# Filler products of ones in TensorE's early waits of a block linear-attention and gated-MLP kernel

## The chip, the core and the metric

The kernel runs on one NeuronCore of a Trainium2 chip. The metric is the device time of one execution in microseconds (us), less being better. Five runs of the kernel before give a median of 153.36 us (153.28 to 153.47).

## What is computed

Two stages in a row. The first is linear attention with decay over 4 batches, 8 heads, 768 tokens and head size 64, in blocks of 64 tokens: inside a block, masked and decayed scores times v; from earlier blocks, q times a running 64x64 state per head. The second is an MLP with a spatial gate on the attention's output (4 x 768 x 512):

```
for b in range(nb):
    intra = einsum('bhic,bhjc->bhij', qb, kb) * Dmask;  intra = einsum('bhij,bhjd->bhid', intra, vb)
    inter = einsum('bhid,bhde->bhie', qb * lam_pow, kv_state)
    out[:, :, sl] = intra + inter
    kv_state = lam_block * kv_state + einsum('bhsd,bhse->bhde', kb * rev_pow, vb)
...
h = maximum(x @ w_in, 0);  u, v = halves of h
v_n = (v - mean) / sqrt(var + 1e-6)
out = (u * (w_spatial @ v_n + b_spatial)) @ w_out
```

## The kernel before, in words

The work is cut into 12 steps n of 256 tokens, three to a batch. For each step q, k and v are loaded (512 KB each, into 3 buffers in turn), cast to bf16, and k and q are transposed on TensorE (TK, TQ, L302) and copied out of PSUM as kT and qT (EK, EQ). Scores are SC (L331), masked on VectorE by MK (L335). AV.n.0 and AV.n.1 (L368 and L377) form the attention output of step n: products of q with the state copied to SBUF, and products of v with the masked scores. KV.n.c (L347) adds block half c of step n to the running state, which lives in the first 256 columns of PSUM bank 7 (`SB`), and SS.n.c (L353, a copy whose line in the profile is its helper's, L170 on ScalarE and L172 on VectorE) copies that state to `s_sb`. AV.n.1 needs the copy SS.n.0. EX evicts AV as xT. Then follow the MLP's products PV (L406, the v half, with eviction EV, statistics BN, RA, RD and normalisation VN), PU (L451, the u half, eviction EU), and later PW (L473, spatial), GB and GM (the gate) and PO (L490, output).

The order of every instruction is written out by hand in the string `ORDER`: each token names a helper, its arguments and its engine (T TensorE, D VectorE, A ScalarE, P GpSimd, S SyncE; `AV.2.1.0.T` is step 2, part 1, bank 0), and each engine takes its own tokens strictly in that order. Waits between engines are made from the tiles that the instructions read and write. For PSUM they are made by bank: a product into a bank waits until an earlier reader of that bank is done, even if it read other columns. The loads of weights are put behind the arrival of certain inputs: GT (L237) is a tiny GpSimd copy that reads one element of an input and so holds GpSimd's queue until that input has landed, and the weight load follows it (WI, L241, two halves of w_in; WS, L246, two halves of w_spatial).

Lines of the order around the change, of the kernel before:

```
KV.0.1.T EX.0.0.0.A SS.0.1.D SC.1.1.2.T SC.1.0.4.T
...
AV.1.0.0.T BN.0.1.D EV.0.0.5.A LQ.4.2.S KV.1.0.T BN.0.0.D TQ.2.6.T SS.1.0.A GT.0.2.P WS.1.P KC.2.2.A
AV.1.1.0.T EQ.2.6.D KV.1.1.T EX.1.0.0.D SS.1.1.A TK.2.6.T EX.1.1.1.A RA.0.A PV.1.1.5.T
...
AV.2.0.0.T VN.1.0.A LV.3.2.S EU.1.1.5.A KV.2.0.T SS.2.0.A KC.3.2.D AV.2.1.0.T
EX.2.0.0.D EX.2.1.1.A TK.3.6.T PV.2.1.5.T
```

Of the kernel before, what the change touches and what calls it, by code (L numbers as in the profile page):

```python
# [9 lines left out]
BF16 = mybir.dt.bfloat16  # L10
# [3 lines left out]


ORDER = """
LK.0.2.S lam.A idn.P LQ.0.2.S msk.P LV.0.2.S LK.1.2.S LB.6.T pos.P mkc.D LN.6.A LQ.1.2.S LL.D KC.0.2.P LX.A
LV.1.2.S TK.0.6.T LT.0.A QC.0.2.D EK.0.6.D TQ.0.5.T LT.1.A LQ.2.2.S EQ.0.5.D GT.2.0.P WI.0.P LT.2.A SC.0.0.0.T
LK.2.2.S SC.0.1.2.T VD.0.2.P MK.0.0.0.D KC.1.2.A MK.0.1.2.D LV.2.2.S TK.1.6.T AV.0.0.0.T QC.1.2.D EK.1.6.A
KV.0.0.T TQ.1.5.T SS.0.0.D AV.0.1.0.T EQ.1.5.D KV.0.1.T EX.0.0.0.A SS.0.1.D SC.1.1.2.T SC.1.0.4.T EX.0.1.1.A  # L20
MK.1.1.2.D LK.3.2.S MK.1.0.4.D GT.2.1.P WI.1.P PV.0.1.6.T VD.1.2.D LQ.3.2.S PV.0.0.5.T EV.0.1.6.A QC.2.2.P
AV.1.0.0.T BN.0.1.D EV.0.0.5.A LQ.4.2.S KV.1.0.T BN.0.0.D TQ.2.6.T SS.1.0.A GT.0.2.P WS.1.P KC.2.2.A
AV.1.1.0.T EQ.2.6.D KV.1.1.T EX.1.0.0.D SS.1.1.A TK.2.6.T EX.1.1.1.A RA.0.A PV.1.1.5.T EK.2.6.D SC.2.1.0.T
SC.2.0.2.T EV.1.1.5.A PV.1.0.6.T MK.2.1.0.D BS.S PU.0.0.5.T RD.0.D EV.1.0.6.A BN.1.1.D GT.2.2.P WS.0.P
VN.0.1.A PU.0.1.4.T BN.1.0.D EU.0.0.5.A VD.2.2.P PU.1.0.6.T VN.0.0.A MK.2.0.2.D EU.0.1.4.A PU.1.1.5.T RA.1.A
EU.1.0.6.A RD.1.D VN.1.1.D AV.2.0.0.T VN.1.0.A LV.3.2.S EU.1.1.5.A KV.2.0.T SS.2.0.A KC.3.2.D AV.2.1.0.T
EX.2.0.0.D EX.2.1.1.A TK.3.6.T PV.2.1.5.T EK.3.6.A PV.2.0.4.T EV.2.1.5.A PU.2.0.6.T BN.2.1.D EV.2.0.4.A
LK.4.2.S WT.1.5.T BN.2.0.D EU.2.0.6.A WT.5.4.T QC.3.2.P EW.1.5.A WT.4.3.T EW.5.4.D WT.0.6.T WT.3.2.T RA.2.A
EW.4.3.D LQ.5.2.S EW.0.6.A WT.2.5.T RD.2.D TQ.3.4.T VN.2.1.D VN.2.0.A QC.4.2.D PU.2.1.6.T EW.2.5.A LK.5.2.S
EQ.3.4.D TQ.4.3.T EW.3.2.A SC.3.0.0.T EQ.4.3.D EU.2.1.6.A SC.3.1.4.T PW.0.1.1.2.T MK.3.0.0.D LV.4.2.S  # L30
PW.0.1.0.6.T VD.3.2.P MK.3.1.4.D PW.0.0.0.3.T LQ.6.2.S GB.0.1.0.6.D GB.0.1.1.2.D PW.0.0.1.5.T KC.4.2.A
GB.0.0.0.3.D GM.0.1.1.P LV.6.2.S GM.0.1.0.D AV.3.0.0.T KV.3.0.T GB.0.0.1.5.D TK.4.6.T GM.0.0.0.P SY.3.0.A
SS.3.0.A PW.0.3.1.5.T EK.4.6.A GM.0.0.1.P LQ.7.2.S PW.0.2.0.4.T GB.0.3.1.5.D QC.5.2.P GM.0.3.1.D KV.3.1.T
AV.3.1.0.T GB.0.2.0.4.D LV.5.2.S KC.5.2.A SC.4.1.2.T SC.4.0.5.T GM.0.2.0.P PW.0.3.0.4.T MK.4.1.2.D EX.3.1.1.A
VD.4.2.P EX.3.0.0.A TK.5.1.T MK.4.0.5.D LK.6.2.S SS.3.1.A TQ.5.3.T EK.5.1.A PU.3.0.0.T EQ.5.3.D QC.6.2.P
PU.3.1.6.T LK.7.2.S GB.0.3.0.4.D EU.3.0.0.A KV.4.0.T GM.0.3.0.P EU.3.1.6.D AV.4.0.0.T SS.4.0.A SC.5.1.2.T
SC.5.0.4.T SY.4.0.D LQ.9.2.S KV.4.1.T MK.5.1.2.D AV.4.1.0.T SS.4.1.A PV.3.1.6.T EX.4.0.0.A VD.6.2.P MK.5.0.4.D
EX.4.1.1.A TQ.6.0.T LV.7.2.S PU.4.1.1.T EV.3.1.6.D QC.7.2.P PU.4.0.5.T EQ.6.0.D EU.4.1.1.A LV.9.2.S BN.3.1.D
PV.4.1.6.T GT.2.5.P WO.P EU.4.0.5.D KC.6.2.A PW.0.2.1.4.T VD.5.2.P EV.4.1.6.D LK.8.2.S TK.6.5.T BN.4.1.D
PV.3.0.6.T EK.6.5.A GB.0.2.1.4.D KV.5.0.T LV.8.2.S EV.3.0.6.D AV.5.0.0.T GM.0.2.1.P SS.5.0.A SC.6.1.2.T  # L40
SC.6.0.4.T SY.5.0.D BN.3.0.D KV.6.0.T AV.5.1.0.T KC.7.2.P PV.4.0.6.T EX.5.0.0.A MK.6.0.4.D EX.5.1.1.A TK.7.0.T
RA.3.A SS.6.0.D PU.5.1.1.T EV.4.0.6.A EK.7.0.D PV.5.1.6.T BN.4.0.D EU.5.1.1.A MK.6.1.2.D TQ.7.0.T LK.9.2.S
RA.4.A EV.5.1.6.A PV.5.0.1.T QM.9.0.P BN.5.1.D PO.0.0.6.T EV.5.0.1.A QM.9.1.P RD.4.D LQ.8.2.S EQ.7.0.D
PO.0.1.5.T VN.4.0.A BN.5.0.D VD.7.2.P EO.0.0.6.A PO.0.2.4.T EO.0.1.5.A VN.4.1.D ST.0.0.S RA.5.A AV.6.0.0.T
EO.0.2.4.A KV.6.1.T SC.7.1.2.T SY.6.0.D RD.5.D SC.7.0.5.T SS.6.1.A KC.8.2.P RD.3.D AV.6.1.0.T MK.7.1.2.D
VN.5.0.A KV.7.0.T PO.0.5.4.T LV.10.2.S EX.6.1.1.A SS.7.0.A MK.7.0.5.D VN.3.1.A PO.0.3.1.T VD.8.2.P EX.6.0.0.D
KV.7.1.T DK.8.S EO.0.3.1.A AV.7.0.2.T VN.3.0.D PU.5.0.6.T SS.7.1.A SY.7.2.A KC.9.2.P VN.5.1.D PV.6.1.5.T
ST.0.1.S EU.5.0.6.D PV.6.0.1.T ST.0.3.S QM.8.1.P EV.6.1.5.D AV.7.1.2.T EV.6.0.1.D QM.8.0.P KV.8.0.T PU.6.0.6.T
EX.7.1.3.A BN.6.1.D LK.11.2.S EX.7.0.2.A VD.9.2.P PW.1.1.1.3.T BN.6.0.D SS.8.0.A EU.6.0.6.A PU.7.1.2.T RA.6.A
DQ.8.S GB.1.1.1.3.D RD.6.D PU.6.1.6.T GM.1.1.1.D VN.6.0.A LQ.11.2.S EU.7.1.2.A EO.0.5.4.D PW.1.0.1.3.T DK.9.S  # L50
EU.6.1.6.A VN.6.1.A PW.1.3.1.2.T GB.1.0.1.3.D ST.0.2.S GM.1.0.1.P PV.7.1.6.T GB.1.3.1.2.D PV.7.0.3.T
# [30 lines left out]
def kernel(  # L82
# [29 lines left out]
    def sb(shape, dt, name):  # L112
        return const.tile(shape, dt, name=name)
# [5 lines left out]
    SB = 7  # L119
# [45 lines left out]
    def bank(b, n=1):  # L165
        return ps[:, b] if n == 1 else ps[:, b:b + n]
# [338 lines left out]
    def st_o(e, bb, t):  # L505
        eng = {"S": nc.sync, "A": nc.scalar}[e]
        eng.dma_start(out=out[bb, t * P:(t + 1) * P, :], in_=o_sb[(bb * NT + t) % NO])

    ops = dict(GT=after, lam=c_lam, pos=c_pos, LB=l_b, LN=l_n, LL=l_l, LX=l_x, LT=l_t, idn=c_ident, msk=c_mask, mkc=c_mask2, WI=w_in, WS=w_sp, WO=w_out, BS=b_sp,
               LK=ld_k, LQ=ld_q, LV=ld_v, KC=k_c, QM=q_m, DK=d_k, DQ=d_q, QC=q_c, VD=v_d, TK=t_k, TQ=t_q, EK=e_k, EQ=e_q,  # L510
               SC=s_c, MK=m_k, KV=k_v, SS=s_s, AV=a_v, SY=s_y, EX=e_x, PV=p_v, EV=e_v, BN=b_n, RA=r_a, RD=r_d,
               VN=v_n, PU=p_u, EU=e_u, WT=w_t, EW=e_w, PW=p_w, GB=g_b, GM=g_m, PO=p_o, EO=e_o, ST=st_o, EH=e_h, SH=s_h)
# [34 lines left out]
```

## Time and profile before

| | before |
|---|---|
| median of 5 runs | 153.36 us |
| the profiled execution's own time | 153.62 us |
| its span, first to last instruction | 151.9 us |
| TensorE products, busy | 132.5 us (87%), 2011 recorded |
| VectorE busy | 110.7 us (73%) |
| ScalarE busy | 85.9 us (57%) |
| GpSimd busy | 71.9 us (47%) |
| mean granted TensorE clock | 0.995 |
| moved by DMA | 30.73 MB, mean 202 GB/s |
| a load of k, q or v, issue to landing | 7.1 us (median) |
| a half of w_in, issue to landing | 9.6 us (median) |

Times in the profile count from the first instruction. A timeline row holds start, duration, engine, source line, operation, output and inputs, shape and how many instructions are merged; in square brackets stands how long the engine was idle before it and what ended the wait. The duration of merged products includes the latency of the last one. "PE" is TensorE, "PEld" its weight loads, "POOL" GpSimd, "DVE" VectorE, "ACT" ScalarE. A few products are missing from the trace. The chain of waits is followed back from the last instruction to what released it, and so on to the start.

### The profile page before, as it was taken

To read this page: it belongs to the slowest core of one execution; us is meant where nothing else is said; L and a number is where in the kernel's file an instruction comes from. 1 tells how busy PE (TensorE), PEld (TensorE's weight loads), DVE (VectorE), ACT (ScalarE), POOL (GpSimd) and SP (SyncE) were. 2 spreads that over 40 slices of the span, in tenths; PEclk is the share of its full clock that TensorE was granted. 3 is DMA by queue.
4 is the path that set the end of the run, shared out by engine and by line. 5 is a ranking of instruction groups with operands and counts; after the bars stand their busy time and mean duration, and the time that the engine had idled before them with its cause. 6 is when DMAs were issued, how large, how long until landed. Compare 5 with 4: busy or idle time off the path is not lost.

```text
span 151.9 us, 4756 instructions
## 1 busy us (share of the span) xinstructions
PE 132.5 (87%) x2011; PEld 87.9 (58%) x2026; DVE 110.7 (73%) x200; ACT 85.9 (57%) x158; POOL 71.9 (47%) x73
## 2 busy tenths in 40 slices
PE   1259498969979999999999999999999999999990
PEld 1248347755855688685656756664576656556530
DVE  3467847764999689999999669976589949535611
ACT  6882237897952474565964732968351777670140
POOL 7472023800404798955888050897384020009720
PEclk9999999999999999999999999999999999999998
DMA  3999999999999996999799999675654010151055
GB/s 105 298 290 249 289 226 292 238 245 303 258 288 293 291 229 185 285 218 306 200 207 299 205 273 297 178 140 110 221 182 46 4 73 0 69 207 71 0 211 207
DMA packets 52040, 30.73 MB, mean 202 GB/s; under 512 B 9522, under 2 KB 48946, under 8 KB 52018
## 3 DMA queue, kind: packets, MB, share of 16 engines
q1 hardware_dynamic: 49488, 27.53, 69.9%
q0 software_dynamic: 2384, 2.75, 10.7%
q8 instruction: 16, 0.26, 0.8%
q10 hardware_dynamic: 146, 0.13, 0.2%
q14 instruction: 6, 0.05, 0.1%
HBM read 24.77 MB, written 6.29 MB: 204 GB/s over the span
## 4 chain that ended last, share of the span: by engine, by line
PE 63%; DMA 12%; DVE 11%; ACT 7%; issue 3%; SPq 1%; POOL 0%; ACTq 0%; DVEq 0%
PE ps L473 20%; PE ps L406 13%; PE ps L451 11%; PE ps L490 8%; DMA win_sb<-in_moe_w_in_dram 6%; DMA v_in<-in_v_dram 4%; PE ps L377 3%; DVE a_sb L335 2%; PE ps L331 2%; PE ps L302 2%; PE ps L347 2%; ACT vn L439 2%; PE ps L368 2%; ACT o_sb L170 2%; DMA out_dram<-o_sb 2%
## 5 line engine op out<-in xcount | busy, mean ns | idle before, releaser
L484 POOL TENSOR_TENSOR gT<-vsb,uT 128x384 bf16<-128x384 f32 x24 | 26.1, 1105 | 42.2 <-DVE vsb L478 41.1
L473 PE MATMUL ps<-wt_sb,vn 128*128 128x384 bf16 x192 | 33.7, 326 | 0.7 <-DVE vsb L478 0.6
L335 DVE TENSOR_TENSOR a_sb<-ps,m 128x1024 bf16<-128x1024 f32 x24 | 28.4, 1213 | 2.3 <-PE ps L331 2.2
L406 PE MATMUL ps<-win_sb,xT 128*128 128x512 bf16 x87 | 23.6, 399 | 3.6 <-DMA win_sb<-in_moe_w_in_dram 1.9
L473 PEld LDWEIGHTS <-vn 128*128 128x128 bf16 x192 | 18.5, 98 | 13.1 <-issue 0.7
L294 POOL TENSOR_TENSOR vd<-v_in,lv 128x1024 bf16<-128x1024 f32 x11 | 21.0, 1906 | 10.8 <-DVE rstd L432 9.5
L478 DVE TENSOR_TENSOR vsb<-ps,bsp 128x384 f32<-128x384 f32 x32 | 17.3, 551 | 9.6 <-PE ps L473 8.5
L451 PE MATMUL ps<-xT,win_sb 128*128 128x256 bf16 x192 | 23.9, 273 | 0.0
L421 DVE BATCH_NORM_STATS2 st<-vh 128x6 f32<-128x512 bf16 x24 | 16.5, 686 | 9.5 <-ACT vh L411 9.2
L490 PE MATMUL ps<-wout_sb,gT 128*128 128x512 bf16 x90 | 21.6, 379 | 0.5 <-issue 0.3
L451 PEld LDWEIGHTS <-win_sb 128*128 128x128 bf16 x192 | 18.4, 98 | 4.2
L170 ACT ACTIVATE o_sb<-ps 128x512 f32<-128x512 f32 (+1 forms) x20 | 11.5, 583 | 14.6 <-PE ps L490 9.9
L170 ACT ACTIVATE xT<-ps 128x512 bf16<-128x512 f32 x21 | 11.6, 592 | 7.7 <-PE ps L377 7.7
L406 PEld LDWEIGHTS <-xT 128*128 128x128 bf16 x96 | 9.1, 101 | 11.8 <-issue 3.6
L439 ACT ACTIVATE vn<-vh,nmr,rstd 128x512 bf16<-128x512 bf16 x16 | 12.8, 812 | 4.9 <-DVE nmr L433 4.9
L411 ACT ACTIVATE vh<-ps 128x512 bf16<-128x512 f32 x15 | 8.9, 593 | 11.3 <-PE ps L406 11.2
L490 PEld LDWEIGHTS <-gT 128*128 128x128 bf16 x96 | 9.1, 98 | 10.3 <-DMA wout_sb<-in_moe_w_out_dram 0.2
L411 ACT ACTIVATE uT<-ps 128x512 bf16<-128x512 f32 x20 | 11.7, 590 | 5.4 <-PE ps L451 5.4
L377 PE MATMUL ps<-a_sb,vd 64*64 64x128 bf16 x384 | 10.8, 229 | 0.1
L331 PE MATMUL ps<-qT,kT 64*64 64x128 bf16 x384 | 9.2, 233 | 0.9 <-DVE qT L315 0.9
L302 PE MATMUL ps<-ident,kc 128*128 128x128 bf16 x64 | 5.7, 242 | 4.6 <-POOL kc L174 3.5
L279 POOL TENSOR_TENSOR qc<-q_in,lqn 128x512 bf16<-128x512 f32 x7 | 7.7, 1116 | 3.3 <-issue 3.3
(68 smaller groups left out, 171.6 us busy)
## 6 DMA issues: line engine op xcount, KB each, us to landing
k_in<-in_k_dram SPq DMA_DIRECT2D x12, 512.0 KB, 7.1
q_in<-in_q_dram SPq DMA_DIRECT2D x12, 512.0 KB, 7.1
v_in<-in_v_dram SPq DMA_DIRECT2D x12, 512.0 KB, 7.1
out_dram<-o_sb SPq DMA_DIRECT2D x23, 256.0 KB, 2.2
wsp_raw<-in_moe_w_spatial_dram POOLq DMA_DIRECT2D x2, 576.0 KB, 9.3
win_sb<-in_moe_w_in_dram POOLq DMA_DIRECT2D x2, 512.0 KB, 9.6
wout_sb<-in_moe_w_out_dram POOLq DMA_DIRECT2D x1, 512.0 KB, 9.1
bsp<-in_moe_b_spatial_dram SPq DMA_DIRECT2D x1, 384.0 KB, 12.3
```

Of the source, the lines that this page charges most:

```text
L170: nc.scalar.activation(out=o, in_=i, func=AF.Copy)
L294: vec(e).tensor_tensor(out=vd[n % NCA][:, h], in0=v_in[n % NIN][:, h], in1=lv[:, n % NR, h].unsqueeze(3).broadcast_to((P, h.stop - h.start ...
L335: nc.vector.tensor_tensor(out=a_sb[n % NA][:, i].rearrange("p o w j x -> p (o w) (j x)"), in0=bank(b, 2).rearrange("p o (w y) -> p (o w) y ...
L406: nc.tensor.matmul(out=bank(b), lhsT=x[:, c, g], rhs=win_sb[:, g, DH:DFF], start=(g == 0), stop=(g == NCH - 1))
L411: nc.scalar.activation(out=o, in_=i, func=AF.Relu)
L421: nc.vector.bn_stats(out=st6[p2][:, t], in_=vh[p2][:, t])
L439: nc.scalar.activation(out=vn[p2][:, t], in_=vh[p2][:, t], func=AF.Identity, scale=rstd[p2][:, t:t + 1], bias=nmr[p2][:, t:t + 1])
L451: nc.tensor.matmul(out=pu[:, f2].rearrange("p (c x) -> p c x", c=2), lhsT=win_sb[:, g, f * P:(f + 1) * P], rhs=x[:, :, g, :], start=(g == ...
L473: nc.tensor.matmul(out=bank(b)[:, 0:HW], lhsT=vn[bb % 2][:, s, f * P:(f + 1) * P], rhs=wt_sb[:, s, i * HW:(i + 1) * HW], start=(s == 0), s ...
L478: nc.vector.tensor_tensor(out=vsb[(bb * 4 + f) % NVS][:, i * HW:(i + 1) * HW], in0=bank(b)[:, 0:HW], in1=bsp[:, i * HW:(i + 1) * HW], op=A ...
L484: vec(e).tensor_tensor(out=gT[bb % 2][:, f, cols].rearrange("p (a y m) -> p a y m", m=2, y=Q64), in0=vsb[(bb * 4 + f) % NVS][:, cols].rear ...
L490: nc.tensor.matmul(out=bank(b), lhsT=gT[bb % 2][:, f, t * P:(t + 1) * P], rhs=wout_sb[:, f, :], start=(f == 0), stop=(f == NCH - 1))
```

## The change

A tile `warm` of 128x128 bf16 is added and filled with 1.0 by one VectorE memset, ahead of the other work of VectorE. A helper WU issues n products of `warm` with itself, each with its own weight load, into columns 256 to 383 of bank 7, which nothing reads. 14 tokens of it, 152 products in all, stand in the order from the start up to step 3; nothing else in the order is moved.

```diff
+    warm = sb([P, P], BF16, "warm")
...
+    def w_u(e, n):
+        if n < 0:
+            nc.vector.memset(warm, 1.0)
+        for x in range(abs(n)):
+            nc.tensor.matmul(out=bank(SB)[:, 4 * D:4 * D + P], lhsT=warm, rhs=warm, start=(n < 0 and x == 0), stop=True,
+                             skip_group_check=True)
```

Where the tokens stand on TensorE (number of products, and what follows them there): 8 before LB.6 (the first product of the kernel, L201), 45 before TK.0, 10 before TQ.0, 12 before SC.0.0, 21 before TK.1, 4 before KV.0.0, 3 before SC.1.1, 22 before PV.0.1, 4 before KV.1.0, 4 before TK.2, 4 before PV.1.1, 4 before KV.2.0, 8 before AV.2.1 and 3 before TK.3.

More of the change, by code (lines that the diff above doesn't have):

```diff
@@ L16 @@
 ORDER = """
[L17 to L46, printed above, removed]
@@ L47 @@
-KV.7.1.T DK.8.S EO.0.3.1.A AV.7.0.2.T VN.3.0.D PU.5.0.6.T SS.7.1.A SY.7.2.A KC.9.2.P VN.5.1.D PV.6.1.5.T
-ST.0.1.S EU.5.0.6.D PV.6.0.1.T ST.0.3.S QM.8.1.P EV.6.1.5.D AV.7.1.2.T EV.6.0.1.D QM.8.0.P KV.8.0.T PU.6.0.6.T
+LK.0.2.S lam.A idn.P LQ.0.2.S msk.P LV.0.2.S LK.1.2.S WU.-8.T LB.6.T pos.P mkc.D LN.6.A LQ.1.2.S LL.D KC.0.2.P
+LX.A LV.1.2.S WU.45.T TK.0.6.T LT.0.A QC.0.2.D EK.0.6.D WU.10.T TQ.0.5.T LT.1.A LQ.2.2.S EQ.0.5.D GT.2.0.P
+WI.0.P LT.2.A WU.12.T SC.0.0.0.T LK.2.2.S SC.0.1.2.T VD.0.2.P MK.0.0.0.D KC.1.2.A MK.0.1.2.D LV.2.2.S WU.21.T
@@ new lines @@
+TK.1.6.T AV.0.0.0.T QC.1.2.D EK.1.6.A WU.4.T KV.0.0.T TQ.1.5.T SS.0.0.D AV.0.1.0.T EQ.1.5.D KV.0.1.T
+EX.0.0.0.A SS.0.1.D WU.3.T SC.1.1.2.T SC.1.0.4.T EX.0.1.1.A MK.1.1.2.D LK.3.2.S MK.1.0.4.D GT.2.1.P WI.1.P
+WU.22.T PV.0.1.6.T VD.1.2.D LQ.3.2.S PV.0.0.5.T EV.0.1.6.A QC.2.2.P AV.1.0.0.T BN.0.1.D EV.0.0.5.A LQ.4.2.S
+WU.4.T KV.1.0.T BN.0.0.D TQ.2.6.T SS.1.0.A GT.0.2.P WS.1.P KC.2.2.A AV.1.1.0.T EQ.2.6.D KV.1.1.T EX.1.0.0.D
+SS.1.1.A WU.4.T TK.2.6.T EX.1.1.1.A RA.0.A WU.4.T PV.1.1.5.T EK.2.6.D SC.2.1.0.T SC.2.0.2.T EV.1.1.5.A
@@ new lines @@
+PV.1.0.6.T MK.2.1.0.D BS.S PU.0.0.5.T RD.0.D EV.1.0.6.A BN.1.1.D GT.2.2.P WS.0.P VN.0.1.A PU.0.1.4.T BN.1.0.D
+EU.0.0.5.A VD.2.2.P PU.1.0.6.T VN.0.0.A MK.2.0.2.D EU.0.1.4.A PU.1.1.5.T RA.1.A EU.1.0.6.A RD.1.D VN.1.1.D
+AV.2.0.0.T VN.1.0.A LV.3.2.S EU.1.1.5.A WU.4.T KV.2.0.T SS.2.0.A KC.3.2.D WU.8.T AV.2.1.0.T EX.2.0.0.D
+EX.2.1.1.A WU.3.T TK.3.6.T PV.2.1.5.T EK.3.6.A PV.2.0.4.T EV.2.1.5.A PU.2.0.6.T BN.2.1.D EV.2.0.4.A LK.4.2.S
+WT.1.5.T BN.2.0.D EU.2.0.6.A WT.5.4.T QC.3.2.P EW.1.5.A WT.4.3.T EW.5.4.D WT.0.6.T WT.3.2.T RA.2.A EW.4.3.D
@@ new lines @@
+LQ.5.2.S EW.0.6.A WT.2.5.T RD.2.D TQ.3.4.T VN.2.1.D VN.2.0.A QC.4.2.D PU.2.1.6.T EW.2.5.A LK.5.2.S EQ.3.4.D
+TQ.4.3.T EW.3.2.A SC.3.0.0.T EQ.4.3.D EU.2.1.6.A SC.3.1.4.T PW.0.1.1.2.T MK.3.0.0.D LV.4.2.S PW.0.1.0.6.T
+VD.3.2.P MK.3.1.4.D PW.0.0.0.3.T LQ.6.2.S GB.0.1.0.6.D GB.0.1.1.2.D PW.0.0.1.5.T KC.4.2.A GB.0.0.0.3.D
+GM.0.1.1.P LV.6.2.S GM.0.1.0.D AV.3.0.0.T KV.3.0.T GB.0.0.1.5.D TK.4.6.T GM.0.0.0.P SY.3.0.A SS.3.0.A
+PW.0.3.1.5.T EK.4.6.A GM.0.0.1.P LQ.7.2.S PW.0.2.0.4.T GB.0.3.1.5.D QC.5.2.P GM.0.3.1.D KV.3.1.T AV.3.1.0.T
@@ new lines @@
+GB.0.2.0.4.D LV.5.2.S KC.5.2.A SC.4.1.2.T SC.4.0.5.T GM.0.2.0.P PW.0.3.0.4.T MK.4.1.2.D EX.3.1.1.A VD.4.2.P
+EX.3.0.0.A TK.5.1.T MK.4.0.5.D LK.6.2.S SS.3.1.A TQ.5.3.T EK.5.1.A PU.3.0.0.T EQ.5.3.D QC.6.2.P PU.3.1.6.T
+LK.7.2.S GB.0.3.0.4.D EU.3.0.0.A KV.4.0.T GM.0.3.0.P EU.3.1.6.D AV.4.0.0.T SS.4.0.A SC.5.1.2.T SC.5.0.4.T
+SY.4.0.D LQ.9.2.S KV.4.1.T MK.5.1.2.D AV.4.1.0.T SS.4.1.A PV.3.1.6.T EX.4.0.0.A VD.6.2.P MK.5.0.4.D EX.4.1.1.A
+TQ.6.0.T LV.7.2.S PU.4.1.1.T EV.3.1.6.D QC.7.2.P PU.4.0.5.T EQ.6.0.D EU.4.1.1.A LV.9.2.S BN.3.1.D PV.4.1.6.T
@@ new lines @@
+GT.2.5.P WO.P EU.4.0.5.D KC.6.2.A PW.0.2.1.4.T VD.5.2.P EV.4.1.6.D LK.8.2.S TK.6.5.T BN.4.1.D PV.3.0.6.T
+EK.6.5.A GB.0.2.1.4.D KV.5.0.T LV.8.2.S EV.3.0.6.D AV.5.0.0.T GM.0.2.1.P SS.5.0.A SC.6.1.2.T SC.6.0.4.T
+SY.5.0.D BN.3.0.D KV.6.0.T AV.5.1.0.T KC.7.2.P PV.4.0.6.T EX.5.0.0.A MK.6.0.4.D EX.5.1.1.A TK.7.0.T RA.3.A
+SS.6.0.D PU.5.1.1.T EV.4.0.6.A EK.7.0.D PV.5.1.6.T BN.4.0.D EU.5.1.1.A MK.6.1.2.D TQ.7.0.T LK.9.2.S RA.4.A
+EV.5.1.6.A PV.5.0.1.T QM.9.0.P BN.5.1.D PO.0.0.6.T EV.5.0.1.A QM.9.1.P RD.4.D LQ.8.2.S EQ.7.0.D PO.0.1.5.T
@@ new lines @@
+VN.4.0.A BN.5.0.D VD.7.2.P EO.0.0.6.A PO.0.2.4.T EO.0.1.5.A VN.4.1.D ST.0.0.S RA.5.A AV.6.0.0.T EO.0.2.4.A
+KV.6.1.T SC.7.1.2.T SY.6.0.D RD.5.D SC.7.0.5.T SS.6.1.A KC.8.2.P RD.3.D AV.6.1.0.T MK.7.1.2.D VN.5.0.A
+KV.7.0.T PO.0.5.4.T LV.10.2.S EX.6.1.1.A SS.7.0.A MK.7.0.5.D VN.3.1.A PO.0.3.1.T VD.8.2.P EX.6.0.0.D KV.7.1.T
+DK.8.S EO.0.3.1.A AV.7.0.2.T VN.3.0.D PU.5.0.6.T SS.7.1.A SY.7.2.A KC.9.2.P VN.5.1.D PV.6.1.5.T ST.0.1.S
+EU.5.0.6.D PV.6.0.1.T ST.0.3.S QM.8.1.P EV.6.1.5.D AV.7.1.2.T EV.6.0.1.D QM.8.0.P KV.8.0.T PU.6.0.6.T
@@ L507, in st_o @@
         eng.dma_start(out=out[bb, t * P:(t + 1) * P, :], in_=o_sb[(bb * NT + t) % NO])
-    ops = dict(GT=after, lam=c_lam, pos=c_pos, LB=l_b, LN=l_n, LL=l_l, LX=l_x, LT=l_t, idn=c_ident, msk=c_mask, mkc=c_mask2, WI=w_in, WS=w_sp, WO=w_out, BS=b_sp,
+    ops = dict(GT=after, lam=c_lam, WU=w_u, pos=c_pos, LB=l_b, LN=l_n, LL=l_l, LX=l_x, LT=l_t, idn=c_ident, msk=c_mask, mkc=c_mask2, WI=w_in, WS=w_sp, WO=w_out, BS=b_sp,
                LK=ld_k, LQ=ld_q, LV=ld_v, KC=k_c, QM=q_m, DK=d_k, DQ=d_q, QC=q_c, VD=v_d, TK=t_k, TQ=t_q, EK=e_k, EQ=e_q,
```

## Prediction

> **What bounds the kernel now.** I read the slices of the page first, then TensorE's timeline over the first 36 us, where all of the new products stand, then the chain of waits, then the landings of the inputs.
>
> The page's slices (3.8 us each) show TensorE busy in patches up to about the tenth slice, the DMA engines full there, and a granted clock that is full in every slice but the last:
>
> ```profile
> PE   1259498969979999999999999999999999999990
> PEclk9999999999999999999999999999999999999998
> DMA  3999999999999996999799999675654010151055
> ```
>
> The clock row doesn't tell the whole story. TensorE's timeline holds the same work twice:
>
> ```profile
> 15.57 1.04 PE L331 MATMUL ps<-qT,kT 64*64 64x128 bf16 x28
> 18.55 0.58 PE L406 MATMUL ps<-win_sb,xT 128*128 128x512 bf16 x1 [1.94 <-DMA win_sb<-in_moe_w_in_dram]
> 19.36 2.76 PE L406 MATMUL ps<-win_sb,xT 128*128 128x512 bf16 x6 [0.22 <-issue]
> ...
> 23.26 1.04 PE L302 MATMUL ps<-ident,qc 128*128 128x128 bf16 x8
> ...
> 25.07 0.61 PE L302 MATMUL ps<-ident,kc 128*128 128x128 bf16 x8
> 26.20 0.81 PE L406 MATMUL ps<-win_sb,xT 128*128 128x512 bf16 x3 [0.52 <-ACT xT L170]
> 26.94 0.64 PE L331 MATMUL ps<-qT,kT 64*64 64x128 bf16 x32
> ```
>
> Eight transposes take 1.04 us at 23.26 and 0.61 at 25.07; 32 score products 0.64 at 26.94 where 28 took 1.04 at 15.57. In w_in's products the pitch is (2.76 - 0.58) / 5 = 0.44 us at 19.36, against 0.22 later (4 in 1.04 us with a latency of 0.38). So TensorE works at half speed until about 24.2 us and at full speed after that. The change fills its waits so that full speed comes earlier. What that is worth depends on which of the slow work lies on the chain:
>
> ```profile
> 8.79 9.72 DMA win_sb<-in_moe_w_in_dram
> ...
> 25.04 0.38 ACT s_sb L170
> 25.43 0.50 ACT xT L170
> 25.93 0.27 issue
> 26.20 0.81 PE ps L406 x3
> ...
> 33.59 0.28 ACT s_sb L170
> 33.87 0.04 issue
> 33.91 0.31 PE ps L368 x8
> ```
>
> Up to 18.51 the chain is a transfer (v of step 0, then w_in). From 18.55 to 25.02 it is TensorE at half speed, then ScalarE and TensorE in turn, and at 33.91 AV.2.1, which waited for the state copy SS.2.0. After that the chain has no input transfer before the end: TensorE, VectorE and ScalarE only. A shift of AV.2.1 therefore goes through to the end nearly unchanged.
>
> The last view is what lands beside this chain:
>
> ```profile
> 23.33 0.18 POOL L237 COPY seen<-k_in 1x1 f32<-1x1 f32 x1 [2.49 <-DMA k_in<-in_k_dram]
> 23.37 0.38 ACT L170 ACTIVATE s_sb<-ps 128x256 bf16<-128x256 f32 x1 [0.61 <-PE ps L347]
> 23.65 1.05 ACT L170 ACTIVATE kc<-k_in 128x1024 bf16<-128x1024 f32 x1
> ```
>
> k of step 2 lands at about 23.3 (GpSimd had waited 2.49 us for it). Its cast KC.2 sits in ScalarE's queue ahead of SS.1.1, EX.1.1, RA.0 and EV.1.1. ScalarE passes 23.3 no earlier however fast TensorE is.
>
> **The change, part by part.**
>
> *The 125 products up to PV.0.1 (8, 45, 10, 12, 21, 4, 3, 22).* Price: they have the shape of the transposes, so 0.113 us each slow ((1.03 - 0.24) / 7, from eight in 1.03) and 0.055 fast (eight start 0.44 us ahead of the next eight around 54 us). At most 125 x 0.113 = 14.1 us, at least 6.9. They run in waits that the timeline shows before the work that they precede (3.47 us before TK.0, 0.40, 0.85, 1.02, then 1.94 before PV.0.1), and they may overrun: 45 x 0.113 = 5.1 us before TK.0 against 3.47 idle, 1.6 late if all are slow. That costs nothing at the end if TensorE, which was done at 16.61, still reaches PV.0.1 by 18.51; once the array is fast, the work between (some 7 us at half speed) gives back over 3 us. The memset costs VectorE some 0.2 us (0.17 for its neighbour) ahead of the wait for the mask; the eight first products end near 2.1, where LB began at 2.11. WU.3 before SC.1.1 inherits a wait for SS.0.1, since both touch bank 7; SC.1.1 then starts up to 0.6 later than now, but runs 0.4 us shorter. All of this lies before 18.51 and is covered by w_in's landing. I take 0; were the cover gone, it would be 1 to 2 us.
>
> Here the Trainium skill ("TensorE: Matmul & The Clock Gate", Part 1) bears on the gain: the array starts at half clock, turns fast after about 3.4 us of sustained work, and for modelling the ramp costs under 1% of a typical span (1.5 us here). The row differs: from 11.55 TensorE was at work nearly without a break to 16.61 and stayed slow. By the rule TensorE would be fast near 7 us; by the slowest row (dense from 18.55, fast at 24.2: 5.6 us) near 8.3. In both cases it is fast by 18.55, which is what matters.
>
> *PV.0.1 to EX.1.1, the gain.* From 18.55 to 25.02 TensorE does some 6.5 us of chain, mostly slow; at full speed it would do it in about 3.5. But KC.2 waits for k. After it: KC.2 23.33 to 24.38 (was 23.65 to 24.70), SS.1.1 at 24.3 (was 25.04, having waited 0.35 for KV.1.1), done near 24.67, EX.1.1 done near 25.2 (was 25.92). So ScalarE gains 0.75 us, not 3. TensorE gains less: the four products before TK.2 write bank 7 after KV.1.1, so in the built program the first of them carries the wait for SS.1.1; before, TK.2 waited for KC.2 only. Start 24.71, four products 0.22, eight transposes 0.44, four products 0.22: PV.1.1 at about 25.6 to 25.65, where it was 26.20. The gain is 0.55 us. EK.2 (VectorE, at 25.6) is ready for SC.2.0, so PV.1.0 keeps the 0.55, and EV.1.0 goes from 28.59 to 28.04. From there the chain is ScalarE back to back to SS.2.0, 33.59 to 33.87: 33.32 in place of 33.87. VD.2, needed by AV.2.0, ends at 29.0 whatever TensorE does (v lands at 25.7), before the 31.4 at which AV.2.0 would come.
>
> *WU.4 before KV.2.0.* 0.22 us; KV.2.0 ended near 32.74 and SS.2.0 began at 33.48, being behind ScalarE's queue: covered.
>
> *WU.8 before AV.2.1, the price.* In the built program the first of the eight carries the wait for SS.2.0, the very copy that AV.2.1 waits for (1.17 us idle in the trace). The eight are thus not in the wait but behind it, and AV.2.1, EX.2.1 and PV.2.1 are queued behind them: 8 x 0.055 = 0.44 us straight on the chain. Ends: 0.44 by the transposes' pitch, 0.78 if each weight load (98 ns in the PEld rows) counts in full. I take 0.44, the row of the same shape.
>
> *WU.3 before TK.3.* 0.17 us; PV.2.1 waits for EX.2.1, with 0.36 us of idle time before it: covered. EK.3 follows 0.1 later on ScalarE, just ahead of EV.2.1.
>
> *Sum.* AV.2.1 at 33.32 + 0.04 + 0.44 = 33.80, where it was 33.91: -0.11 us. The profiled execution took 153.62 us (span 151.9 and 1.7 around it) and would take 153.51; it lies 0.26 above the median of the runs, so against the median 153.36 - 0.11 = 153.25.
>
> **The rivals.**
>
> *Clearly faster.* ScalarE's gain of 0.75 reaches SS.2.0 in full, because PV.1.1 is released by EX.1.1 and not by the products ahead of it: -0.75 + 0.44 = -0.31, so 153.05; with a little more from looser ordering after step 3, 152.9. For it: the chain from 25.04 runs through EX.1.1. Against it: in the sum TensorE arrives 0.15 to 0.2 after EX.1.1. Chance 0.25.
>
> *Slower.* The eight products behind SS.2.0 keep their price, and the gain before them is lost on the way: SS.2.0 is held by ScalarE's full queue from 28.59, and if EV.1.0 comes no earlier (bank waits, VectorE's masks and RD.0 ahead of VN.0.1), the price stands alone: +0.44, 153.80. It decides as soon as SS.2.0 gains less than 0.13 us. Against it: each link in front is TensorE or ScalarE work that moves with the clock. Chance 0.12.
>
> *The clock doesn't hold.* With the work before k's landing done early, TensorE idles from about 22.5 to 24.7, 2.2 us; the longest idle time that the trace shows at full speed up to 60 us is 1.2. If the array fell to half speed there, the 3 us of work to PV.1.0 would take 2.3 us or more extra: 155. The skill (same page, "Why this matters for your kernels") lets gaps below about 3 us pass, which would leave the sum as it is; no row here shows a gap of 2.2. I follow the rule: 0.06.
>
> **How the numbers follow.** A measurement of this kernel can tell about 0.2% (0.31 us) from no change: within 153.05 to 153.67 is "same". The likeliest case, with the gain 0.2 us and the price 0.1 us to either side (152.95 to 153.55), holds 0.57; faster 0.25; slower 0.12 + 0.06 = 0.18. The range takes in the faster rival's 152.85 and the upper side of the price to 153.75, and leaves out the lone price of the slower one and the clock's case.
>
> **What would show it.** Right: eight transposes in 0.61 us near 7 to 9; the four products of PV.0.1 in about 1.0 us from 18.55; KC.2 at 23.33 and PV.1.1 near 25.6; the eight products starting right after SS.2.0 near 33.3 and AV.2.1 0.45 later. Wrong: w_in or k landing at another time; transposes at 1.03 still after 18; SS.2.0 earlier than 32.9 (a gain I missed); AV.2.1 starting at once after SS.2.0; a new wait after 36.

## The result, and the profile after

The median fell from 153.49 us (44 runs) to 152.89 us (25 runs): ratio 0.9959, interval 0.9948 to 0.9971, so 0.6 us faster. The profiled execution took 152.98 us (span 151.3), against 153.62 (151.9). The prediction had 153.25 with 152.85 to 153.75: the time lies inside the range, near its lower end, below the likeliest case's 152.95, where the rival "clearly faster" (chance 0.25) had its 152.9. The change is 0.6 us where the sum had 0.11, and the trace shows that the sum was wrong in how it came to its number, too. In what follows some executions of a kernel show the array at half speed for one further stretch of 3.4 us; the mean granted clock of each execution tells of such a fall (a slow start it doesn't show).

Slices of the page of after (tenths; slices of 3.8 us):

```profile
PE   7988698869989999999999999999999999999990
```

TensorE is busy from the first slice. Its timeline in after (start, duration, what):

```profile
6.37 0.61 PE L311 MATMUL ps<-ident,kc 128*128 128x128 bf16 x8
...
24.65 0.81 PE L415 MATMUL ps<-win_sb,xT 128*128 128x512 bf16 x3
...
33.87 0.61 PE L205 MATMUL ps<-warm 128*128 128x128 bf16 x8 [0.98 <-ACT s_sb L172]
34.41 0.31 PE L377 MATMUL ps<-qT,s_sb 64*64 64x128 bf16 x8
```

The first eight transposes take 0.61 us at 6.37: the array is at full speed 18 us earlier than before. PV.1.1 starts at 24.65, 1.55 us earlier than in before, where 0.55 was predicted. Yet the eight products behind SS.2.0 start at 33.87, where before had AV.2.1 at 33.91. The gain was lost between these two rows. The chain of waits of after says where:

```profile
27.26 1.75 DVE nmr L442
...
29.10 0.81 ACT vn L448
...
33.87 0.61 PE ps L205 x8
```

`nmr` is new on the chain. It is the last line of RD (L433 before, L442 after): one VectorE instruction over 128x2 numbers, -mean x rstd, which VN on ScalarE takes as its bias. The timelines of all engines show why an instruction over two columns takes 1.74 us. First before:

```profile
27.10 1.91 POOL L294 TENSOR_TENSOR vd<-v_in,lv 128x1024 bf16<-128x1024 f32 x1
...
28.81 0.23 DVE L433 SCALAR_TENSOR_TENSOR nmr<-mv,rstd 128x2 f32<-128x2 f32 x1
...
39.92 1.90 POOL L294 TENSOR_TENSOR vd<-v_in,lv 128x1024 bf16<-128x1024 f32 x1 [9.46 <-DVE rstd L432]
39.94 2.03 DVE L442 TENSOR_SCALAR vn<-vh,mv,rstd 128x512 bf16<-128x512 bf16 x1
```

and after:

```profile
27.06 1.92 POOL L303 TENSOR_TENSOR vd<-v_in,lv 128x1024 bf16<-128x1024 f32 x1
27.26 1.74 DVE L442 SCALAR_TENSOR_TENSOR nmr<-mv,rstd 128x2 f32<-128x2 f32 x1
...
39.48 1.90 POOL L303 TENSOR_TENSOR vd<-v_in,lv 128x1024 bf16<-128x1024 f32 x1 [3.44 <-DMA v_in<-in_v_dram]
...
40.36 1.05 DVE L442 SCALAR_TENSOR_TENSOR nmr<-mv,rstd 128x2 f32<-128x2 f32 x1
41.33 0.40 DVE L451 TENSOR_SCALAR vn<-vh,mv,rstd 128x512 bf16<-128x512 bf16 x1
```

Add start and duration in each pair. VD.2, a GpSimd product, ends at 29.01 before and 28.98 after; `nmr` ends at 29.04 and 29.00, whether it started at 28.81 or at 27.26. Free of such company it takes 0.16 us. The same happens at VD.3: in before VN.2.1 starts beside it and is stretched from about 0.41 to 2.03 us (to 41.97), in after `nmr` is stretched to 41.41 and VN.2.1 ends at 41.73. So there are two places where VectorE stands still until a GpSimd product is over. I call them holds. VD.2 stands behind v of step 2, which GpSimd read at 25.8 in both kernels, and behind the issue of a weight load that follows on GpSimd to 27.0. VD.3 starts 0.16 us after v of step 3 has landed (39.76 in before, 39.32 in after, by the landing events of the trace), although the row of before names a VectorE instruction as the last to be waited for; the 0.16 is the same in all nine profiles whose VD.3 is left as it is. Neither place follows TensorE's clock: with full speed from 24.2, 15.7 and 15.5 us in three profiles of before VD.2 starts at 27.10, 27.07 and 27.25 and VD.3 at 39.92, 39.61 and 39.69.

The same instructions matched in the two profiles, after minus before, in us:

| place | shift |
|---|---|
| SS.1.1 (ScalarE, after KC.2) | -1.93 |
| PV.1.1, EV.1.0, start of `nmr` (step 0) | -1.55 |
| end of that `nmr`, VN.0.1, SS.2.0 | -0.04 |
| AV.2.1, EX.2.1, PV.2.1 (behind the eight) | +0.50 |
| end of VN.2.1 (hold of VD.3) | -0.24 |
| 47 to 74 us | -0.45 |
| 76 to 148 us | -0.25 |
| end of the last eviction to the end of the span | 3.12 to 2.71: -0.41 |

### The profile page after: what moved, and what is told of

Same layout as the page of the kernel before. It is cut to its first block, busy times and chain, and to the rows that moved or that the text cites. A ratio compares the mean times of both kernels' runs of the same rounds, so it can differ in the third digit from the quotient of the medians.

```text
span 151.3 us, 5061 instructions
## 1 busy us (share of the span) xinstructions
PE 138.8 (92%) x2163; PEld 94.4 (62%) x2178; DVE 111.7 (74%) x201; ACT 86.2 (57%) x158; POOL 71.9 (48%) x73
## 3 DMA queue, kind: packets, MB, share of 16 engines
q0 software_dynamic: 2384, 2.75, 10.5%
## 4 chain that ended last, share of the span: by engine, by line
PE 64%; DVE 12%; DMA 11%; ACT 7%; issue 2%; SPq 1%; POOL 0%; ACTq 0%; DVEq 0%
PE ps L482 20%; PE ps L415 11%; PE ps L499 11%; PE ps L460 11%; DMA win_sb<-in_moe_w_in_dram 7%; DMA v_in<-in_v_dram 4%; DVE nmr L442 3%; DVE a_sb L344 3%; ACT vn L448 3%; PE ps L386 2%; PE ps L356 2%; PE ps L340 2%; PE ps L311 2%; PE ps L377 2%; DVE vsb L487 2%
## 5 line engine op out<-in xcount | busy, mean ns | idle before, releaser
L482 PEld LDWEIGHTS <-vn 128*128 128x128 bf16 x192 | 18.6, 98 | 12.9 <-issue 0.3
L415 PE MATMUL ps<-win_sb,xT 128*128 128x512 bf16 x87 | 22.1, 379 | 2.3 <-DMA win_sb<-in_moe_w_in_dram 1.4
L172 ACT ACTIVATE o_sb<-ps 128x512 f32<-128x512 f32 (+1 forms) x20 | 11.6, 584 | 14.5 <-PE ps L499 10.3
L205 PE MATMUL ps<-warm 128*128 128x128 bf16 x152 | 12.5, 239 | 3.1 <-ACT s_sb L172 1.5
L420 ACT ACTIVATE vh<-ps 128x512 bf16<-128x512 f32 x15 | 8.9, 594 | 11.1 <-PE ps L415 11.1
L205 PEld LDWEIGHTS <-warm 128*128 128x128 bf16 x152 | 10.4, 108 | 3.7 <-issue 1.9
L386 PE MATMUL ps<-a_sb,vd 64*64 64x128 bf16 x384 | 10.2, 217 | 0.4 <-DVE a_sb L344 0.3
L176 POOL CAST qc<-q_in 128x1024 bf16<-128x1024 f32 x5 | 5.2, 1033 | 9.1 <-DMA q_in<-in_q_dram 6.0
```

The costliest lines, as they stand in the source:

```text
L172: nc.scalar.activation(out=o, in_=i, func=AF.Copy)
L205: nc.tensor.matmul(out=bank(SB)[:, 4 * D:4 * D + P], lhsT=warm, rhs=warm, start=(n < 0 and x == 0), stop=True, skip_group_check=True)
L415: nc.tensor.matmul(out=bank(b), lhsT=x[:, c, g], rhs=win_sb[:, g, DH:DFF], start=(g == 0), stop=(g == NCH - 1))
L420: nc.scalar.activation(out=o, in_=i, func=AF.Relu)
L482: nc.tensor.matmul(out=bank(b)[:, 0:HW], lhsT=vn[bb % 2][:, s, f * P:(f + 1) * P], rhs=wt_sb[:, s, i * HW:(i + 1) * HW], start=(s == 0), s ...
```

## The theories and the experiments

The theory of the prediction, C in the texts below: the time follows the clock, each shift on TensorE before AV.2.1 goes through to the end, and the eight products cost 0.44. The rival, H: the holds of VD.2 and VD.3 absorb every shift in front of them, gains as well as prices, and what is left at the end is where the landing of v puts VD.3. R: the gain is a by-product of where the loads happen to land. None of the kernels leaves out any of the reference's work; products of `warm` are read by nobody.

A table of the runs first. Kernels of one group ran on one chip with the same runs of the kernel before.

| kernel | median us (executions) | before beside it | AV.2.1 starts | VN.2.1 ends |
|---|---|---|---|---|
| before again | 153.50 (12) | 153.52 | | 41.85 |
| after again | 152.78 (12) | 153.52 | | 41.69 |
| after without the eight | 152.90 (12) | 153.52 | 34.00 | 41.91 |
| before with only the eight | 153.49 (12) | 153.52 | 34.09 | 41.92 |
| thin products | 153.27 (12) | 153.73 | | |
| wide products | 154.94 (12) | 153.73 | | |
| before, VD.3 later | 154.70 (12) | 153.73 | | 41.84 |
| after without eight, both moves | 151.75 (5) | 153.73 | 32.41 | 38.85 |
| before, both moves | 155.95 (6) | 153.51 | | |
| after, both moves | 152.45 (9) | 153.51 | | |
| after without eight, both moves, one-input `nmr` | 150.18 (6) | 153.51 | | |

In the first group four of the 35 executions of the kernel before lie at 150.70 to 152.34, and the ratio of the kernel before to itself came out as 1.011 (1.006 to 1.016); there I compare medians.

**The two kernels again.** No edit.

> The kernel before, unchanged: a second profile, to see which of the landings repeat. Theory H (hold and landing: the end follows the GpSimd product VD.3, which starts when v of step 3 lands and holds VectorE till it ends, at 41.8 us; a landing is moved by when TensorE's instructions are fetched): v of step 1 lands again near 14.0, k of step 2 near 23.3, v of step 3 near 39.8, the first 16 KB fetch of instructions comes near 16.4, and VN.2.1 ends near 42.0. Chance theory R (the landings change from execution to execution, whatever the kernel): they lie about half a microsecond or more elsewhere. Time ratio 1.000 within 0.001.

> The changed kernel again. Theory H: the first fetch near 11.5, v of step 1 landing near 15.4, k of step 2 near 21.5, v of step 3 near 39.3, nmr of step 0 stretched to the end of VD.2 near 29.0, VN.2.1 ending near 41.7; time 0.996 of before. Chance theory R: landings in other places, and the time ratio depends on them. Clock theory C (the prediction's: the end moves with TensorE's and ScalarE's chain up to AV.2.1): cannot tell from this run why AV.2.1 is 0.5 us later and the end 0.6 earlier.

Medians 153.50 and 152.78: the gain is there again, 0.7 us here. This second profile of before is an experiment by itself: its array reached full speed at 15.7 instead of 24.2 (28 score products in 0.61 us where the first profile had 1.04), and it had EV.1.0 1.25 us earlier, with no filler. Its `nmr` started at 27.55, took 1.46 us and ended at 29.01; VN.2.1 ended at 41.85, 0.12 earlier. An early clock alone, and nearly all of it is gone at VD.2:

```profile
15.69 0.61 PE L331 MATMUL ps<-qT,kT 64*64 64x128 bf16 x28
...
27.07 1.91 POOL L294 TENSOR_TENSOR vd<-v_in,lv 128x1024 bf16<-128x1024 f32 x1
27.55 1.46 DVE L433 SCALAR_TENSOR_TENSOR nmr<-mv,rstd 128x2 f32<-128x2 f32 x1
```

In the second profile of after `nmr` stood still from 26.78, 0.22 before VD.2's recorded start (27.00), while GpSimd was still issuing a weight load; so a hold may begin with that, and these runs don't separate the two. A third profile of the kernel before:

> The kernel before once more, for a third profile of it. If the 0.4 us more between the last eviction and the end in its first profile is chance: 3.2 us there, as in the other profiles. If it belongs to the kernel: 3.6 us again. VN.2.1 ends with VD.3, 41.7 to 42.0.

153.76 us, full speed from 15.5, VN.2.1 to 41.93, VD.3 from 39.69: again early clock and no gain.

**The eight products by themselves.** First after without them, then before with only them (and the memset).

```diff
-KV.2.0.T SS.2.0.A KC.3.2.D WU.8.T AV.2.1.0.T
+KV.2.0.T SS.2.0.A KC.3.2.D AV.2.1.0.T
```

> The changed kernel without the eight products ahead of AV.2.1. Clock theory C: their price (measured 0.54 us from SS.2.0 to AV.2.1) goes, 0.5 us faster than the changed kernel, ratio to before about 0.9925. Theory H: AV.2.1 comes 0.5 us earlier (33.9), but the 0.5 is taken up again by the hold of VD.3 to about 41.4, so the time is as the changed kernel's within 0.1 us, ratio 0.996.

AV.2.1 started at 34.00, 0.41 us earlier than in after, as the prediction's price says. But VD.3 ran 39.67 to 41.57, `nmr` beside it was stretched from 39.96 to 41.59, and VN.2.1 ended at 41.91, later than in after.

```profile
39.67 1.90 POOL L303 TENSOR_TENSOR vd<-v_in,lv 128x1024 bf16<-128x1024 f32 x1 [3.47 <-DMA v_in<-in_v_dram]
...
39.96 1.63 DVE L442 SCALAR_TENSOR_TENSOR nmr<-mv,rstd 128x2 f32<-128x2 f32 x1
```

Median 152.90 against 152.78: C expected about 0.5 us less and falls here.

```diff
-EU.1.1.5.A KV.2.0.T SS.2.0.A KC.3.2.D AV.2.1.0.T
+EU.1.1.5.A KV.2.0.T SS.2.0.A KC.3.2.D WU.8.T AV.2.1.0.T
```

> The kernel before with the memset and only the eight products ahead of AV.2.1. Clock theory C: 0.5 us slower than before, ratio 1.003. Theory H: AV.2.1 near 34.4, but VN.2.1 still ends with VD.3 near 42.0, no change of time (ratio 1.000 within 0.001).

The eight started at 33.56, AV.2.1 at 34.09, 0.53 later; VN.2.1 ended at 41.92, and the median is 153.49 against 153.52. The price is real on TensorE and absent at the end.

**Clock against number of instructions.** Thin products keep the 152 instructions and do next to nothing in each; wide ones are half as many (78), twice as long.

```diff
-nc.tensor.matmul(out=bank(SB)[:, 4 * D:4 * D + P], lhsT=warm, rhs=warm, ...)
+nc.tensor.matmul(out=bank(SB)[:, 4 * D:4 * D + H], lhsT=warm[0:1, :], rhs=warm[0:1, 0:H], ...)
```

> The changed kernel with each of its 152 products cut to one row and 8 columns of ones (same number of TensorE instructions, same places, hardly any work for the array). Theory H (the end follows the landing of v of step 3 and GpSimd's holds; landings move because the extra 304 instructions bring the first 16 KB fetch forward): fetch near 11 to 13, v of step 1 late (near 15), k of step 2 near 21.5, v of step 3 near 39.4; ratio 0.996, whatever the clock does. Clock theory C: if the array stays slow up to about 16 to 24 as before, no gain, ratio 1.000.

```diff
-warm = sb([P, P], BF16, "warm")
+warm = sb([P, 2 * P], BF16, "warm")
-for x in range(abs(n)): nc.tensor.matmul(out=bank(SB)[:, 4 * D:4 * D + P], lhsT=warm, rhs=warm, ...)
+for x in range((abs(n) + 1) // 2): nc.tensor.matmul(out=bank(SB)[:, 4 * D:4 * D + 2 * P], lhsT=warm[:, 0:P], rhs=warm, ...)
```

> The changed kernel with half as many products of twice the width (256 columns): the array is kept as busy, with 77 products in place of 152 and half the extra instructions. Clock theory C: full speed from about 5 to 7 us as in the changed kernel, ratio 0.996. Theory H: the first fetch lies between the two kernels' (about 13 to 14), so it meets another load, and the landings are those of before or in between; ratio 0.998 to 1.000.

Thin: full speed only from 22.2, and 153.27 (ratio 0.9967, 0.9937 to 0.9996). Wide: full speed from 7.6, and 154.94 (1.0060, 1.0032 to 1.0088). In ten of the wide kernel's twelve executions the mean granted clock was 0.989 or less, a later fall to half speed; the other two took 153.85 and 153.55, no faster than before. The eight executions of the thin kernel that kept theirs (0.997 or more) have a median of 153.02. So a late clock with many instructions gained, by little over its interval, and an early clock with half of them did not at the end. Part of the way it did: in the profile of the wide kernel (153.85, without a fall) everything from 52 to 68 us stands 0.44 us earlier than in before, as in after; this and more, 1.1 us, was lost from 68 to 72 us, 0.90 of it in a wait of TensorE (68.26 to 69.16) for which the trace names no cause. Something else than the clock goes with the number of instructions: in the thin kernel v of step 1 was read at 15.52 and k of step 2 at 21.90, as in after (15.51, 21.53); in before at 14.12 and 23.33; in the wide kernel v of step 1 at 14.22 and k at 22.30. Over 14 profiles there is no exception: in kernels with 144 or more added products the first instruction block, one packet of 16,384 bytes that keeps a DMA engine for about 1 us, is fetched at 11.1 to 12.2 us, v of step 1 lands at 15.0 to 15.6 and k of step 2 is read at 21.4 to 21.9. In kernels with eight or none it is fetched at 16.4 to 16.8, and these are 14.0 to 14.2 and 22.2 to 23.7. The wide kernel fetches it at 14.5 and has these as in the second group. Before fetches 16 such blocks, after 17. 152 products with their weight loads are 304 instructions. The Trainium skill ("Runtime: NRT & Kernel Launch", Instruction fetch mechanics) has streams refilled in blocks of 16 KiB, 256 instructions, mostly hidden. The size of the block and the one more of them agree with 304 more instructions; that the fetch costs something here, namely shifts these loads, by 1.4 us for v, is the likely reading, not a tested one.

**Taking a hold away.** To keep VD.3 off the critical instructions, GpSimd first reads one element of QC.4, a later VectorE cast:

```diff
+def q_w(e, n): nc.gpsimd.tensor_copy(out=seen[:, 0:1], in_=qc[n % NCA][0:1, 0, 0, 0, 0:1])
-VD.3.2.P MK.3.1.4.D
+QW.4.P VD.3.2.P MK.3.1.4.D
```

> The kernel before, and on GpSimd a one-element read of the cast QC.4 ahead of VD.3, so that VD.3 starts when VectorE has passed VN.2.1 and QC.4. Theory H: VN.2.1 takes 0.4 us in place of 2.0 and ends near 40.4, QC.4 near 41.1, VD.3 runs 41.2 to 43.1 (AV.3.0 needs it at 46 only); 1.2 to 1.6 us earlier at 47, at the end 0.8 to 1.5 us faster, ratio 0.990 to 0.995. Theory C and any in which the long duration of VN.2.1 has another cause: no change or slower by up to 0.3 us.

The hold was gone: VD.3 started at 42.72 and VN.2.1 took 0.41 us. But the median rose to 154.70 (1.0054, 1.0028 to 1.0081), where I had expected 0.990 to 0.995. The stretches of this kernel, with TensorE's busy time first and the granted clock in the column after POOL, show why:

```profile
31.50:34.90 3.40, 1.89 (x72) 1.39 (x64) 1.90 (x6) 2.78 (x7) 1.04 (x1) 1.00 1.14 252
34.90:38.30 3.40, 3.28 (x8) 1.19 (x9) 0.90 (x2) 1.64 (x3) 0.00 (x0) 0.50 1.15 320
```

After a stretch in which TensorE was busy for 1.89 of 3.40 us the array ran the next 3.4 us at half speed, BN came 1.5 us late, and that ate what the hold had cost (VN.2.1 ends 0.13 earlier than in before). Then at 75.57 another `nmr` stood still for 1.75 us beside a GpSimd product, and the shift against before went from +0.12 to +1.61 us. The fall isn't all of it: the two executions that kept their clock took 154.39 and 154.73, so this second hold, or something that the profile doesn't show, has a share. The kernel before falls too: in 47 of the 78 executions beside these experiments its mean granted clock was 0.99 or less, and these have a median of 153.72, the others 153.56. The fall costs it little; that the hold covers it is what this suggests.

**Both holds away, with the fillers, and without.** After without the eight, with RD.0 put ahead of VectorE's mask MK.2.1, so that `nmr` is done before VD.2 begins, and with the edit above:

```diff
-PV.1.0.6.T MK.2.1.0.D BS.S PU.0.0.5.T RD.0.D EV.1.0.6.A
+PV.1.0.6.T RD.0.D MK.2.1.0.D BS.S PU.0.0.5.T EV.1.0.6.A
```

> The changed kernel without the eight products ahead of AV.2.1, with RD.0 moved ahead of MK.2.0 (so that nmr of step 0 is done before VD.2 takes GpSimd) and VD.3 behind QC.4 as in the run before. Theory H: with both holds gone TensorE's early clock is worth something at last: SS.2.0 1.3 to 1.9 us earlier, VN.2.1 ending near 39 to 40, the end 1.5 to 2.5 us before the kernel before's, ratio 0.984 to 0.990, if no landing (wsp at 35.3, k of step 4 at 41.1) stops it. Theory C: only the eight's price, ratio about 0.993.

151.75 (0.9863, 0.9833 to 0.9893). `nmr` takes 0.18 us at 25.93, VD.2 follows at 27.16, AV.2.1 starts at 32.41 (33.91 in before), VN.2.1 ends 3.12 us earlier than in before and at 74 us the gain is still 2.88. There the next hold stands, in the timeline of this kernel:

```profile
72.41 1.90 POOL L306 TENSOR_TENSOR vd<-v_in,lv 128x1024 bf16<-128x1024 f32 x1
72.57 1.76 DVE L445 SCALAR_TENSOR_TENSOR nmr<-mv,rstd 128x2 f32<-128x2 f32 x1
```

`nmr` ends at 74.33, with the GpSimd product (74.31). This takes 1.5 us back, and 1.38 remain. The same two moves in the order of the kernel before, without fillers:

> The kernel before (no products of ones) with both moves of the run without holds: RD.0 ahead of MK.2.0, VD.3 behind QC.4. Theory H1 (the holds were the whole bound, the array's early clock is worth nothing): 151.8, as with the products. Theory H2 (once the holds are gone the early clock counts: half speed until 16 to 24 us, and in many executions for another 3.4 us later, now reach the end): 152.5 to 154, 0.8 us or more slower than the run without holds.

155.95, slower than before. The profiled execution has the array at half speed at 18.6 to 22.0, after a stretch with TensorE busy 0.89 of 3.40 us, and again at 35.7 to 39.1 after one with 1.39. In the kernel with fillers it was busy 2.23 us in 15.2 to 18.6 and 3.29 in 32.3 to 35.7, and none of its five executions fell. So once the moves are made the medians with and without fillers lie 155.95 - 151.75 = 4.2 us apart. By an estimate, two stretches of 3.4 us, busy throughout at half speed, do 3.4 us less of work. But that isn't a price of the clock alone. The first hold also stayed in this kernel: without the early k its `nmr` came to 27.31 and took 1.82 us, and as it now stood ahead of the masks, AV.2.0 waited 1.19 us for one (to 33.04), a wait that the kernel with fillers doesn't have. Of the six executions two kept their clock; they took 152.19 and 154.86, 0.4 and 3.1 us more than with fillers. So the 4.2 us hold for the kernels as they usually run, and how they divide between clock and hold is open. And the eight, put back into the kernel without holds (the two edits above, applied to after):

> The run without holds, but with the eight products ahead of AV.2.1 put back. If their price of 0.5 us was only hidden by the hold of VD.3: AV.2.1 and VN.2.1 0.5 us later than in the run without holds, 152.2. If a later hold (near 72 to 76, nmr against KC.8 and VD.8) takes it up: 151.75, with VN.2.1 0.5 later and the rest level from 76.

152.45 (0.9918, 0.9889 to 0.9947). The shift at 47 to 74 us is -2.53 where it was -2.88, and -1.03 at the end where it was -1.38: their price, 0.35 us, now goes through to the end in these two profiles. The medians of the two kernels differ by 0.7, over two chips. One of the nine executions fell in its clock (0.989) all the same and took 155.82.

**The instruction that is held.** `nmr` read two SBUF tensors. Written for each column with a per-partition scalar it reads one:

```diff
-nc.vector.scalar_tensor_tensor(out=nmr[p2][:, pair], in0=mv[p2][:, pair, 0], scalar=-1.0, in1=rstd[p2][:, pair], ...)
+for t in (2 * r, 2 * r + 1):
+    nc.vector.tensor_scalar(out=nmr[p2][:, t:t + 1], in0=mv[p2][:, t, 0:1], scalar1=rstd[p2][:, t:t + 1], scalar2=-1.0, ...)
```

> The run without holds, with nmr (L433: two operands from SBUF, minus mean times 1/std) written as two products with a per-partition scalar, one tensor operand each. If what lets GpSimd hold nmr is its second tensor operand: no nmr of 0.7 to 1.8 us is left near 69, 72 and 105, 0.5 to 1.5 us faster than the run without holds, 150.3 to 151.3. If any VectorE operation there is held: the two are stretched the same way, 151.75 or up to 0.2 slower.

150.18 us (0.9767, 0.9724 to 0.9811), the fastest version of all, 3.3 us below the kernel before beside it. VectorE and GpSimd of this kernel:

```profile
69.42 1.90 POOL L306 TENSOR_TENSOR vd<-v_in,lv 128x1024 bf16<-128x1024 f32 x1
...
70.40 1.08 DVE L455 TENSOR_SCALAR vn<-vh,mv,rstd 128x512 bf16<-128x512 bf16 x1
...
71.47 1.04 POOL L176 CAST kc<-k_in 128x1024 bf16<-128x1024 f32 x1
...
71.64 0.33 DVE L446 TENSOR_SCALAR nmr<-mv,rstd 128x1 f32<-128x1 f32 x2
```

The pair at 71.64 runs freely beside a GpSimd cast; in the kernel without holds the old `nmr` took 0.74 us at this place (71.72), up to the end of the same cast. None of the 24 small instructions takes over 0.22 us, where the longest of the 12 old ones took 1.76. VN, a bf16 instruction over 512 columns, is still stretched, to 1.08 us. This is what the Trainium skill says ("SBUF — State Buffer", SBUF: two separate sides): VectorE and GpSimd share a pair of ports as an exclusive lock for a whole instruction, which VectorE needs in a 2-port mode or for two inputs from SBUF. The trace agrees for `nmr` and for its one-input form; that VN runs in a 2-port mode is the page's side of it, and no run here shows it apart.

## Why the prediction was right or wrong

The sign came out, and the time lies in the range, but the change was 0.6 us where the sum had 0.11, and it did not come by the sum's way: of the gain in front, 1.55 us in place of 0.55, only 0.04 passed the hold of VD.2, and the price behind it, 0.50 us, was gone after the hold of VD.3. That the time fell into the range is luck.

**The clock, right.** Full speed before 7 us, transposes in 0.61, and nothing lost by the 125 products before PV.0.1 against the first profile (w_in landed within 0.2 us of its old time). The two other profiles of before had w_in at 17.2, though, where those with 144 or more fillers had it at 18.2 to 18.9; this landing was no fixed point either. "The clock doesn't hold" fell: with k earlier, TensorE was busy for 2.92 of the 3.40 us up to 24.0, idle for 0.48 before the four products, and no execution of after has a mean granted clock below 0.995.

**"ScalarE passes 23.3 no earlier however fast TensorE is", wrong.** It took k's landing as fixed. GpSimd read k of step 2 at 21.53, so KC.2 began at 22.13 and PV.1.1 gained 1.55 us in place of 0.55. The number of TensorE's instructions goes with where loads land, and the prediction priced the added instructions as time on TensorE only.

**"From there the chain is ScalarE back to back to SS.2.0, 33.59 to 33.87: 33.32", wrong.** This is the step that failed most. The gain at EV.1.0 was three times as large as predicted, and 0.04 us of it reached SS.2.0. The prediction knew that VD.2 ends at 29.0, and asked only whether AV.2.0 needs its output. The cost was on the other side: an instruction that needs nothing from VD.2 stands still beside it. In before `nmr` already ended at 29.04, with VD.2 (29.01). An earlier start that still lies beside VD.2, which runs from 27.1, can gain next to nothing.

**The eight products, right in kind, 0.54 in place of 0.44.** From the start of the eight to AV.2.1: 34.41 - 33.87, against a pitch of 0.055 and a handover of 0.04 for AV.2.1 in before; taken out, they gave 0.41, in a profile in which SS.2.0 came 0.13 later.

**The rival "slower" had its mechanism right.** It decides "as soon as SS.2.0 gains less than 0.13 us"; SS.2.0 gained 0.04 and AV.2.1 started 0.50 us later than before. By the prediction's own rule the result was then 153.8.

**"A shift of AV.2.1 therefore goes through to the end nearly unchanged", wrong.** +0.50 at AV.2.1 became -0.24 at VN.2.1. Taken out or put in alone, the eight did not move the end, and with VD.3 out of the way 0.35 us of them did, in one profile each. "After that the chain has no input transfer" looked only at the rows on the chain; v of step 3 acts on it through GpSimd and VectorE's hold.

**What stays open.** Where the 0.6 us come from. The two first profiles place -0.24 at VD.3's hold, which started 0.44 us earlier, and -0.41 in the last store. Neither is settled as an effect of the fillers. The second profile of before is itself 0.20 us ahead of the first from 80 to 140 us, as much as the second of after (0.20). VD.3 starts at 39.61 to 39.92 in four profiles with eight or no fillers and at 39.45 to 39.67 in five with more: these ranges overlap. The last stretch was 3.12, 2.75 and 3.00 us in three profiles of before and 2.71 to 2.73 in after's, but 2.71 also with only the eight. What is shown: the gain repeats, the eight have no part in it, and an early clock as it came by itself in two profiles of before does not bring it. Of the theories, C falls with the eight. The holds of H are shown; that VD.3's start decides the end is not, as the wide kernel has VN.2.1 at 41.74, as in after (41.73), and is no faster than before. Of R it is shown that landings of inputs go with the kernel and not with chance, and not that they make the gain.

## What to carry to other kernels

Before a shift is followed to the end, look for the next place behind it where an engine waits for something that the shift doesn't move: here the landing of v, a GpSimd product and a VectorE instruction stretched to its end. A gain or a price in front of such a place is worth what is left behind it, which can be nothing, and a gain from better clocking can lie hidden until the place is cleared. A VectorE instruction of a few columns that takes over a microsecond and ends with a GpSimd instruction is such a place; here a place ahead of the GpSimd product brought it to 0.18 us, and one SBUF input to 0.21.

## What the runs showed of the hardware

The array lost its speed without a long idle gap. In the stretch of 1.89 busy us shown above, the longest idle time of TensorE was 1.43 us (before AV.2.1). The Trainium skill ("TensorE: Matmul & The Clock Gate", Why this matters for your kernels) lets gaps below about 3 us pass; by that rule this kernel would have kept its clock. The measurement decides: here the array fell after stretches of 1.89 and 1.39 us busy in 3.40 with no gap over 1.43 and 1.27, after one of 0.89 with a gap of 2.51, and once, in the thin kernel, after 2.56, which counts products that do hardly anything. Others passed: 2.23 in before (from 31.00), and 1.56 of 3.41 us in the second profile of before (from 22.47). So the busy time alone doesn't tell, and where the boundary lies these runs don't show.

The same kernel also speeds up at different times: before reached full speed at 24.2, 15.7 and 15.5 us in three profiles. The traces show what these have in common. In the trace's record of the clock its changes within an execution lie multiples of 3.41 us apart, and in all 14 profiles TensorE is busy without a break in the 3.41 us in front of full speed. Counted back in such steps, the work of the first profile of before from 11.55 to 16.61 is split over two stretches, 2.39 busy us from 10.51 and 2.69 from 13.92, and the first full one is 20.75 to 24.16; in the second profile 12.24 to 15.65 is full. So the 9 us between them are likely a matter of where the steps fall. A full stretch is not always enough: in the thin kernel the one from 11.97, thin products included, brought no full speed.
